# Chunked attention and two dense blocks on one core: the last block's weight residuals on VectorE, and matmuls of zeros at the start

## Chip, core and metric

One core of one Trainium2 chip. The metric is the device time of one execution in microseconds, the median of several; lower is better. TensorE is called PE in the profile, VectorE DVE, ScalarE ACT, GpSimd POOL, and SyncE, which issues all DMA transfers here, SP.

## The reference

Inputs are q, k, v of shape (4, 8, 576, 64), float32. Attention stays inside chunks of 64 positions. Its output, as 2304 tokens of 512 features, goes through two dense blocks with 512 -> 2048 -> 512 weights:

```python
scores = scale * np.matmul(q_c, k_c.transpose(0, 1, 2, 4, 3))   # per chunk of 64
attn = softmax(scores)
x = transpose(attn @ v_c)                       # (2304, 512)
h = x @ w_in;   g = h * np.clip(h + 3.0, 0.0, 6.0) / 6.0;               x = g @ w_out
h = x @ w_in2;  g = np.maximum(h, 0.0) + np.log1p(np.exp(-np.abs(h)));  return g @ w_out2
```

## The kernel before

**Pieces and steps.** The tokens are cut into five pieces: piece 0 of 256 tokens, pieces 1 to 4 of 512. The hidden dimension of 2048 is cut into 16 slices f of 128. A step is one (layer, piece, f): `first_product` (L786) makes 128 hidden rows of h for the piece with 12 matmuls, `activate` (L811) turns them into g, and `second_product` (L896) adds the slice's share of the output with up to 12 more. Products are made of two float32r parts each: every operand is split into a high part and the remainder, and hi·hi, lo·hi and hi·lo are added up. For weights, `split` (L337) makes `wh` by a copy on ACT and `wl` by the subtraction w - wh (`less`, L267). wh0 and wl0 belong to the first product's weights, wh1 and wl1 to the second's. The first product needs wh first (L796) and wl in its last four matmuls (L803). For the second product the output is a PSUM bank per 128 tokens: y for 512-token pieces, z for piece 0 (L922).

**The order of the steps** is written at L743 to L754. The one that matters is the end, layer 2: pieces 1, 2 and 3 one after another, 16 slices each, and then, called the last block here, pieces 4 and 0 alternating over f. One round of the last block is a step of 512 tokens and one of 256. On PE the first product of a step runs two steps ahead of the second one (L1055 to L1068).

**The softplus of layer 2** in the last block (L838 to L882): ACT takes abs of h (L844), exp (L853) and Ln (L856). DVE makes d (L859), l - d (L864), r = min(l, 0) + r (L868). In the 512-token step a separate `top` = max(h, 0) is taken from PSUM (L849) and added (L874); in the 256-token step one instruction does both (L879). Then ACT copies g into gh (L263) and gl = g - gh is made on POOL or DVE (L268).

**Who decides the order on the engines.** The program creates jobs and `Schedule.run` (L58) places them: it simulates engines with estimated costs, picks for each engine the job with the earliest due time among those that are ready, and for a job that can run on several engines (`either`, L257) the first listed engine that meets the due time. The result is one fixed instruction list per engine, which runs in order; the semaphores are added from data and buffer dependences. In this model instructions marked as shared on DVE and POOL exclude each other (`begin`, L101).

**The start.** DMA loads q and k of pieces 0 and 1 (`load_nat`, L985). PE transposes them with an identity matrix, for piece 0 at L423, for piece 1 at L430; ACT copies the result to `qkT`; scores follow at L469; softmax uses DVE and ACT. The weights arrive as raw words, and ACT (L302, L305), DVE (L308 to L319) and POOL (L325) convert them; the first block of them is loaded during the attention.

Of the kernel before, what the change touches and what calls it, by code (L numbers as in the profile page):

```python
# [8 lines left out]
F32 = mybir.dt.float32  # L9
F32R = mybir.dt.float32r  # L10
# [160 lines left out]
def kernel(  # L171
# [18 lines left out]
    nc = tc.nc  # L190
    B, H, S, D = q.shape
    NT, DM = out.shape
    DFF = w_in1.shape[1] // 2
    P = 128
# [12 lines left out]
    NPC = len(pieces)  # L207
# [18 lines left out]
    sch = Schedule(bufs)  # L226
# [12 lines left out]
    def act(n, sbuf=False, wide=False):  # L239
        return {"ACT": ((0.205 if sbuf else 0.170) + 0.000833 * n + (0.03 if wide else 0.0), False)}  # L240

    def dve(n, shared=False):
        return {"DVE": (0.155 + n / 960.0, shared)}
# [4 lines left out]
    def pool(n):  # L248
        return {"POOL": (0.205 + 0.00209 * n, True)}
# [4 lines left out]
    def sp(n_bytes, rate):  # L254
        return {"SP": (n_bytes / rate, "dma")}

    def either(*ons):  # L257
        return {e: c for on in ons for e, c in on.items()}


    def copy(e, out, in_):
        if e == "ACT":
            nc.scalar.activation(out=out, in_=in_, func=AF.Copy)  # L263
        else:
            nc.vector.tensor_copy(out, in_)

    def less(e, out, in0, in1):  # L267
        (nc.vector if e == "DVE" else nc.gpsimd).tensor_tensor(out=out, in0=in0, in1=in1, op=ALU.subtract)  # L268
# [65 lines left out]
        w_done[layer, f, i] = sch.job(total, pool(DM), (c, b), (g, w))  # L334
        return ld

    def split(layer, f, i, before):  # L337

        w = w_buf[layer, f, i]
        hi, lo = (Buf(f"{m}{i}", [P, DM], F32R, f"{m}{i}") for m in ("wh", "wl"))  # L340
        a = sch.job(
            lambda e: copy(e, hi.tile, w.tile.bitcast(F32)),
            act(DM, True), (w_done[layer, f, i], before), (w, hi),
        )
        b = sch.job(
            lambda e: less(e, lo.tile, w.tile.bitcast(F32), hi.tile.bitcast(F32)),
            either(pool(DM), dve(DM, True)), (a,), (w, hi, lo),
        )
        return hi, lo, a, b

# [9 lines left out]
    def load_v(x, c, deps=(), due=1e9):  # L360

        t = Buf("x4_1" if (x, c) == (1, 1) else "v", [P, 2, DM], F32, "v")
        for g in range(2):
            for off, m, b, s in runs(x, (2 * c + g) * P, P):
                def load(e, off=off, m=m, b=b, s=s, g=g):
                    nc.sync.dma_start(  # L366
                        out=t.tile[off:off + m, g, :].rearrange("p (h d) -> p h d", h=H),
                        in_=v[b, :, s:s + m, :].rearrange("h p d -> p h d"),
                    )
                v_load.setdefault((x, 2 * c + g), []).append(sch.job(load, sp(m * DM * 4, 218e3), deps, (t,)))  # L370
            v_buf[x, 2 * c + g] = t
# [3 lines left out]
    class Unit:  # L375
# [34 lines left out]
        def load_nat(self, nat):  # L410

            qkT = Buf(("qkT", "raw"), [P, 2, 512], F32, "qkT")
            self.turned = []
            for y in range(2):
                buf, loads = nat[y]
                t = Buf(self.banks, [P, 512], F32, "pb")

                def turn(e, buf=buf, t=t):
                    if self.x == 0:
                        for u, pr in enumerate(self.prs):  # L420
                            for g in range(2):
                                c = (u * 2 + g) * P
                                nc.tensor.transpose(  # L423
                                    t.tile[:, c:c + P], buf.tile[:, g, pr * P:(pr + 1) * P], ident
                                )
                        return
                    cols = t.tile.rearrange("p (n e) -> p n e", e=4)
                    for g in range(4):
                        for par in range(2):
                            nc.tensor.matmul(  # L430
                                out=cols[par * CH:(par + 1) * CH, :, g],
                                lhsT=buf.tile[:, 2 * self.prs[0] + par, g * D:(g + 1) * D], rhs=ident,
                                start=True, stop=True,
                            )
                a = sch.job(
                    turn, {"PE": (0.53 if self.x == 0 else 1.0, False)}, list(loads) + [made_ident], (buf, t)
                )
                self.turned.append(sch.job(
                    lambda e, t=t, y=y: copy(e, qkT.tile[:, y, :], t.tile),
                    either(act(512), dve(512)), (a,), (t, qkT),  # L440
                ))
            self.qkT = qkT
# [320 lines left out]
    def when(layer, x, nth=0):  # L763
        return [s.at for s in steps if (s.layer, s.x) == (layer, x)][nth]
# [3 lines left out]
    last_split = [None, None]  # L768
# [8 lines left out]
    def weights(s, i):  # L777

        key = s.layer, s.f
        if set_now.get(i, (None,))[0] != key:  # L780
            hi, lo, a, b = split(s.layer, s.f, i, last_split[i])
            last_split[i] = a
            set_now[i] = key, (hi, lo, a, b)
        return set_now[i][1]
# [197 lines left out]
    nat0 = [Buf(t, [P, 2, DM], F32, "nat") for t in ("x2_0", "raw")]  # L982
    nat1 = [Buf(t, [P, H, 4 * D], F32, "nat") for t in ("x2_1", "x3_0")]

    def load_nat(buf, src, x, hs):  # L985

        (b, s, m), = pieces[x]
        nh = hs.stop - hs.start
        if x:
            def load(e):  # L990
                nc.sync.dma_start(
                    out=buf.tile[:, hs], in_=src[b, hs, s:s + m, :].rearrange("h (p e) d -> p h (e d)", p=P)
                )
            return [sch.job(load, sp(m * nh * D * 4, 340e3), (), (buf,))]
        got = []
        for g in range(m // P):
            def load(e, g=g):
                nc.sync.dma_start(
                    out=buf.tile[:, g, hs.start * D:hs.stop * D].rearrange("p (h d) -> p h d", d=D),
                    in_=src[b, hs, s + g * P:s + (g + 1) * P, :].rearrange("h p d -> p h d"),  # L1000
                )
            got.append(sch.job(load, sp(P * nh * D * 4, 218e3), (), (buf,)))
        return got

    first = when(1, 0)
    for u in range(2):
        un = Unit(0, (2 * u, 2 * u + 1), first - 0.3, ("y0", "y1", "y2", "y3", "A0", "H0", "A1", "H1"), True)
        hs = slice(4 * u, 4 * u + 4)
        un.load_nat([
            (nat0[y], load_nat(nat0[y], src, 0, hs))  # L1010
            for y, src in enumerate((q, k))
        ])
    load_v(0, 0)
    for un in units:
        un.attend()
    join = when(1, 1)
    for u in range(NP):
        un = Unit(1, (u,), join - 0.3, ("A0", "y0", "y1", "y2", "y3"), True)
# [17 lines left out]
    before = [j for un in units for j in un.turned]  # L1036
    for x in range(2, NPC):
        a, b = when(1, x - 1), when(1, x)
# [5 lines left out]
        for un in us:  # L1044
            un.load(before)
            before = un.loads
# [8 lines left out]
    for i in range(-2, NS):  # L1055
        if i + 2 < NS:
            s = steps[i + 2]
# [51 lines left out]
```

## Time and profile before

| | |
|---|---|
| time, median of 3 (lowest to highest) | 875.54 us (874.14 to 876.92) |
| profiled execution | 875.73 us |
| its span, first to last instruction | 873.9 us |
| busy: PE, DVE, ACT, POOL | 854.6, 606.5, 539.7, 443.9 us |
| mean granted TensorE clock | 0.994 |

The span is what the trace covers; the time holds 1.8 us more. A busy PE means that matmuls are in flight, not that they follow each other as fast as they can: their ends are modelled. The granted clock is a share of 2.4 GHz. A bracket at the end of a row tells how long the engine stood idle before it and which instruction or transfer ended that.

### The profile page before, as it was taken

To read this page: it belongs to the slowest core of one execution; us is meant where nothing else is said; L and a number is where in the kernel's file an instruction comes from. 1 tells how busy PE (TensorE), PEld (TensorE's weight loads), DVE (VectorE), ACT (ScalarE), POOL (GpSimd) and SP (SyncE) were. 2 spreads that over 40 slices of the span, in tenths; PEclk is the share of its full clock that TensorE was granted. 3 is DMA by queue.
4 is the path that set the end of the run, shared out by engine and by line. 5 is a ranking of instruction groups with operands and counts; after the bars stand their busy time and mean duration, and the time that the engine had idled before them with its cause. 6 is when DMAs were issued, how large, how long until landed. Compare 5 with 4: busy or idle time off the path is not lost.

```text
span 873.9 us, 13785 instructions
## 1 busy us (share of the span) xinstructions
PE 854.6 (98%) x5112; PEld 707.8 (81%) x5112; DVE 606.5 (69%) x951; ACT 539.7 (62%) x993; POOL 443.9 (51%) x349
## 2 busy tenths in 40 slices
PE   7899999999999999999999999999999999999996
PEld 6778788888888888888887888888888888888885
DVE  4898899966554645489788555655565556877775
ACT  4865566455444555488777666666666666565654
POOL 0256454644444444479986444444444444655451
PEclk9899999999999999999999999999999999999999
DMA  9872444142112300046730000100010001000002
GB/s 228 269 203 71 147 123 121 25 74 45 23 23 41 66 25 25 20 154 190 209 128 1 1 1 0 49 1 1 0 49 1 1 0 49 1 1 1 1 0 73
DMA packets 101571, 53.33 MB, mean 61 GB/s; under 512 B 76672, under 2 KB 95104, under 8 KB 101504
## 3 DMA queue, kind: packets, MB, share of 16 engines
q1 hardware_dynamic: 101504, 52.45, 22.0%
q8 instruction: 40, 0.66, 0.3%
q14 instruction: 27, 0.22, 0.1%
HBM read 47.71 MB, written 4.72 MB: 60 GB/s over the span
## 4 chain that ended last, share of the span: by engine, by line
PE 73%; DVE 10%; ACT 5%; SPq 4%; POOL 3%; DMA 2%; issue 2%; DVEq 0%; POOLq 0%; ACTq 0%
PE y L922 33%; PE h L796 24%; PE h L803 12%; DVE r L868 3%; PE z L922 2%; DVE l L864 2%; POOL wl L268 2%; DVE r L874 1%; POOL gl L268 1%; ACT r L853 1%; DMA raww<-in_moe_w_in_dram 1%; SPq L395 1%; ACT l L856 1%; ACT r L844 1%; SPq L366 1%
## 5 line engine op out<-in xcount | busy, mean ns | idle before, releaser
L268 POOL TENSOR_TENSOR wl<-w,wh 128x512 fp32r<-128x512 f32 x249 | 329.4, 1325 | 303.8 <-ACT wh L263 235.3
L796 PE MATMUL h<-x,wh 128*128 128x512 f32 (+1 forms) x1280 | 291.4, 370 | 3.0 <-DVE r L834 2.0
L796 PEld LDWEIGHTS h<-x,wh 128*128 128x128 f32 x1280 | 226.3, 189 | 46.6 <-DVE r L834 3.0
L263 ACT ACTIVATE wh<-w 128x512 fp32r<-128x512 f32 x256 | 160.6, 628 | 109.7 <-PE y L922 61.6
L803 PE MATMUL h<-x,wl 128*128 128x512 f32 (+1 forms) x640 | 159.5, 371 | 0.0
L803 PEld LDWEIGHTS h<-x,wl 128*128 128x128 f32 x640 | 113.3, 189 | 19.9
L325 POOL TENSOR_TENSOR w<-w,cg 128x512 int32<-128x512 int32 x64 | 86.2, 1351 | 77.0 <-DVE cg L319 61.5
L263 ACT ACTIVATE gh<-h 128x512 fp32r<-128x512 f32 x96 | 57.4, 597 | 63.5 <-DVE h L879 34.0
L268 DVE TENSOR_TENSOR gl<-h,gh 128x512 fp32r<-128x512 f32 x96 | 66.1, 688 | 43.5 <-ACT gh L263 42.5
L859 DVE TENSOR_SCALAR d<-r 128x512 f32<-128x512 f32 x80 | 33.2, 415 | 75.9 <-ACT r L853 75.8
L868 DVE SCALAR_TENSOR_TENSOR r<-l,r 128x512 f32<-128x512 f32 x80 | 76.6, 958 | 4.8
L834 DVE SCALAR_TENSOR_TENSOR h<-r,h 128x512 f32<-128x512 f32 x48 | 33.2, 692 | 65.6 <-ACT r L827 65.6
L922 PE MATMUL y<-wh,gh 128*128 128x512 f32 x256 | 72.4, 396 | 1.6 <-ACT gh L263 1.0
L922 PE MATMUL y<-gh,wl 128*128 128x512 f32 x256 | 71.4, 393 | 0.2 <-POOL wl L268 0.2
L922 PE MATMUL y<-gl,wh 128*128 128x512 f32 x256 | 70.8, 391 | 0.0
L922 PE MATMUL y<-gh,wh 128*128 128x512 f32 x256 | 70.8, 391 | 0.0
L922 PE MATMUL y<-wl,gh 128*128 128x512 f32 x256 | 70.5, 390 | 0.0
L922 PE MATMUL y<-wh,gl 128*128 128x512 f32 x256 | 70.5, 390 | 0.0
L827 ACT ACTIVATE r<-h 128x512 f32<-128x512 f32 (+1 forms) x80 | 44.1, 552 | 37.0 <-PE h L803 36.8
L263 ACT ACTIVATE gh<-r 128x512 fp32r<-128x512 f32 (+1 forms) x64 | 33.4, 522 | 53.1 <-DVE r L874 22.9
L864 DVE TENSOR_TENSOR l<-l,d 128x512 f32<-128x512 f32 x80 | 53.6, 670 | 14.7 <-ACT l L856 12.8
L922 PEld LDWEIGHTS y<-wh,gh 128*128 128x128 f32 x256 | 47.4, 188 | 15.8 <-ACT gh L263 5.5
(90 smaller groups left out, 1134.6 us busy)
## 6 DMA issues: line engine op xcount, KB each, us to landing
raww<-in_moe_w_in_dram SPq DMA_DIRECT2D x32, 512.0 KB, 3.9
raww<-in_moe_w_out_dram SPq DMA_DIRECT2D x32, 512.0 KB, 4.6
v<-in_v_dram SPq DMA_DIRECT2D x16, 256.0 KB, 4.5
out_dram<-o SPq DMA_DIRECT2D x16, 256.0 KB, 2.0
raw<-in_q_dram SPq DMA_DIRECT2D x32, 64.0 KB, 3.3
raw<-in_k_dram SPq DMA_DIRECT2D x32, 64.0 KB, 2.5
nat<-in_q_dram SPq DMA_DIRECT2D x4, 256.0 KB, 4.2
nat<-in_k_dram SPq DMA_DIRECT2D x4, 256.0 KB, 4.5
```

Source lines behind the costliest of these rows:

```text
L263: nc.scalar.activation(out=out, in_=in_, func=AF.Copy)
L268: (nc.vector if e == "DVE" else nc.gpsimd).tensor_tensor(out=out, in0=in0, in1=in1, op=ALU.subtract)
L325: nc.gpsimd.tensor_tensor(out=w.tile, in0=w.tile, in1=g.tile.bitcast(I32), op=ALU.add)
L366: nc.sync.dma_start(out=t.tile[off:off + m, g, :].rearrange("p (h d) -> p h d", h=H), in_=v[b, :, s:s + m, :].rearrange("h p d -> p h d"),)
L796: nc.tensor.matmul(out=h.tile[:, :n], lhsT=hi.tile[:, kk * P:(kk + 1) * P], rhs=x.tile[:, kk, :], start=(kk == 0 and m == 0), stop=False,)
L803: nc.tensor.matmul(out=h.tile[:, :n], lhsT=lo.tile[:, kk * P:(kk + 1) * P], rhs=xh.tile[:, kk, :], start=False, stop=(kk == KD - 1),)
L827: nc.scalar.activation(out=of(r), in_=of(h), func=AF.Relu, bias=3.0)
L834: lambda e: nc.vector.scalar_tensor_tensor(out=of(g), in0=of(r), scalar=6.0, in1=of(h), op0=ALU.min, op1=ALU.mult), dve(n), (j,), (h, r), due,
L859: lambda e: nc.vector.tensor_scalar(out=of(d), in0=of(r), scalar1=1.0, scalar2=1.0, op0=ALU.add, op1=ALU.subtract), dve2(n), (u,), (r, d),
L864: lambda e: nc.vector.tensor_tensor(out=of(l), in0=of(l), in1=of(d), op=ALU.subtract),
L868: lambda e: nc.vector.scalar_tensor_tensor(out=of(r), in0=of(l), scalar=0.0, in1=of(r), op0=ALU.min, op1=ALU.add), dve(n, not stays), (j,) ...
L922: nc.tensor.matmul(out=bank.tile[:, col:col + width], lhsT=lhs, rhs=rhs, start=(s.first and m == 0 and opens), stop=(s.last and m == 2 and ...
```

## The change

Two things. In the last block the subtraction that makes wl has to run on DVE; before, POOL came first and DVE second in the list. This holds for every split that a step of piece 0 or 4 in layer 2 asks for: 16 slices of two weights, 32 instructions. And at the start a buffer of zeros is made on DVE, six 128x512 matmuls of it go ahead of everything on PE, and a seventh goes between the transposes of q and of k in the first unit. Their results are not used.

```diff
-    def split(layer, f, i, before):
+    def split(layer, f, i, before, beside):
...
         b = sch.job(
             lambda e: less(e, lo.tile, w.tile.bitcast(F32), hi.tile.bitcast(F32)),
-            either(pool(DM), dve(DM, True)), (a,), (w, hi, lo),
+            dve(DM, True) if beside and layer == 2 else either(pool(DM), dve(DM, True)), (a,), (w, hi, lo),
         )
...
-            hi, lo, a, b = split(s.layer, s.f, i, last_split[i])
+            hi, lo, a, b = split(s.layer, s.f, i, last_split[i], s.x in (0, NPC - 1))
...
+    zero, cold = Buf("gl", [P, 512], F32R, "zero"), Buf("H1", [P, 512], F32, "cold")
+    none = sch.job(lambda e: nc.vector.memset(zero.tile.bitcast(F32), 0.0), {"DVE": (0.485, False)}, (), (zero,), 0.0)
+
+    def warm(n, deps, due):
+        def run(e):
+            for _ in range(n):
+                nc.tensor.matmul(out=cold.tile, lhsT=zero.tile[:, :P], rhs=zero.tile, start=True, stop=True)
+        return sch.job(run, {"PE": (0.44 * n, False)}, deps, (zero, cold), due)
+
+    warm(6, [none], 0.0)
...
+        if u == 0:
+            warm(1, un.turns[:1], 0.0)
```

`un.turns` holds the transposing jobs of a unit, the one of q first. In the changed kernel the lines up to 412 keep their numbers, those of `load_nat` are one higher, those from there to `activate` two higher (L844 becomes L846, L868 becomes L870).

The list of PE before, at its beginning:

```order
L423 MATMUL pb<-ident,nat 128x128 x8
L430 MATMUL pb<-ident,nat 64x128 x8
L469 MATMUL ss<-qkT 64x64 x16
```

And of the change:

```order
L994 MATMUL cold<-zero 128x512 x6
L424 MATMUL pb<-ident,nat 128x128 x4
L994 MATMUL cold<-zero 128x512
L424 MATMUL pb<-ident,nat 128x128 x4
L431 MATMUL pb<-ident,nat 64x128 x8
```

Seven matmuls are added; all the rest of PE's list, and that of SP, is in the same order as before.

The list of DVE before, one round in the middle of the last block, with the engines that each instruction waits for:

```order
L849 TENSOR_SCALAR top<-h 128x512 [waits PE_49]
L859 TENSOR_SCALAR d<-r 128x512 [waits Activation_49]
L864 TENSOR_TENSOR l<-l,d 128x512 [waits DVE_49,Activation_49]
L868 SCALAR_TENSOR_TENSOR r<-l,r 128x512 [waits DVE_49,Pool_49]
L874 TENSOR_TENSOR r<-top,r 128x512 [waits DVE_49]
L859 TENSOR_SCALAR d<-r 128x256 [waits Activation_49]
L864 TENSOR_TENSOR l<-l,d 128x256 [waits DVE_49,Activation_49]
L868 SCALAR_TENSOR_TENSOR r<-l,r 128x256 [waits DVE_49,Pool_49]
L879 SCALAR_TENSOR_TENSOR r<-h,r 128x256 [waits DVE_49]
```

And of the change, the same round from its d on (w_7_0 is slice 7 of the first product's weights, w_6_1 slice 6 of the second's):

```order
L866 TENSOR_TENSOR l<-l,d 128x512 [waits DVE_49,Activation_49]
L870 SCALAR_TENSOR_TENSOR r<-l,r 128x512 [waits DVE_49,Pool_49]
L876 TENSOR_TENSOR r<-top,r 128x512 [waits DVE_49]
L268 TENSOR_TENSOR wl_8102<-w_7_0_4710,wh_8096 128x512 [waits PE_49,Activation_49]
L861 TENSOR_SCALAR d<-r 128x256 [waits Activation_49]
L866 TENSOR_TENSOR l<-l,d 128x256 [waits DVE_49,Activation_49]
L870 SCALAR_TENSOR_TENSOR r<-l,r 128x256 [waits DVE_49,Pool_49]
L881 SCALAR_TENSOR_TENSOR r<-h,r 128x256 [waits DVE_49]
L268 TENSOR_TENSOR wl_8137<-w_6_1_4808,wh_8125 128x512 [waits Activation_49]
L851 TENSOR_SCALAR top<-h 128x512 [waits Activation_49]
```

Two wl stand in each round, and top waits for ACT, whose abs reads the same bank of h, where it waited for PE. POOL's list, which had wl, gl of 512, wl, gl of 256 in a round, keeps the two gl.

The list of ACT before, in the same place:

```order
L263 ACTIVATE gh<-r 128x512 [waits DVE_49]
L263 ACTIVATE wh_8033<-w_5_1_4747 128x512 [waits PE_49]
L263 ACTIVATE gh<-r 128x256 [waits DVE_49]
L844 ACTIVATE r<-h 128x512 [waits DVE_49,Pool_49]
L853 ACTIVATE r<-r 128x512 [waits Activation_49]
```

And of the change:

```order
L263 ACTIVATE gh<-r 128x512 [waits DVE_49]
L263 ACTIVATE wh_8043<-w_5_1_4757 128x512 [waits PE_49]
L263 ACTIVATE gh<-r 128x256 [waits DVE_49]
L846 ACTIVATE r<-h 128x512 [waits PE_49,Pool_49]
L855 ACTIVATE r<-r 128x512 [waits Activation_49]
```

The order is the same; abs of the 512-token step waits for PE and POOL instead of DVE and POOL.

## Rows read from the trace of the kernel before

**Rows 1.** The page, busy us (share of the span) and instructions of each engine.

```profile
PE 854.6 (98%) x5112; PEld 707.8 (81%) x5112; DVE 606.5 (69%) x951; ACT 539.7 (62%) x993; POOL 443.9 (51%) x349
```

**Rows 2.** Timeline of PE, last block: start us, us, engine, line, instruction, count [idle].

```profile
762.51 1.07 PE L922 MATMUL y<-wh,gh 128*128 128x512 f32 x4
...
770.77 1.07 PE L922 MATMUL y<-wh,gh 128*128 128x512 f32 x4
...
779.06 1.19 PE L922 MATMUL y<-wh,gh 128*128 128x512 f32 x4
...
787.68 1.20 PE L922 MATMUL y<-wh,gh 128*128 128x512 f32 x4
...
856.43 1.07 PE L922 MATMUL y<-wh,gh 128*128 128x512 f32 x4
...
863.08 0.50 PE L922 MATMUL y<-wh,gh 128*128 128x512 f32 x1 [0.95 <-ACT gh L263]
```

**Rows 3.** Groups by line and shape, 735 to 862 us: count, busy us, mean ns, idle before.

```profile
L268 POOL TENSOR_TENSOR wl<-w,wh 128x512 fp32r<-128x512 f32 x28 | 39.4, 1407 | 21.7 <-ACT wh L263 21.7
...
L868 DVE SCALAR_TENSOR_TENSOR r<-l,r 128x256 f32<-128x256 f32 x15 | 22.8, 1517 | 1.5
...
L868 DVE SCALAR_TENSOR_TENSOR r<-l,r 128x512 f32<-128x512 f32 x15 | 19.6, 1303 | 1.5
...
L268 POOL TENSOR_TENSOR gl<-r,gh 128x256 fp32r<-128x256 f32 x15 | 11.1, 738 | 1.6 <-ACT gh L263 1.6
```

**Rows 4.** Timeline of all engines, block's start and one round of the last block.

```profile
731.00 0.69 DVE L868 SCALAR_TENSOR_TENSOR r<-l,r 128x512 f32<-128x512 f32 x1
...
796.39 1.30 POOL L268 TENSOR_TENSOR gl<-r,gh 128x512 fp32r<-128x512 f32 x1 [2.08 <-ACT gh L263]
796.42 1.54 DVE L868 SCALAR_TENSOR_TENSOR r<-l,r 128x256 f32<-128x256 f32 x1
...
799.12 0.60 ACT L844 ACTIVATE r<-h 128x512 f32<-128x512 f32 x1 [0.24 <-POOL wl L268]
...
801.64 1.29 POOL L268 TENSOR_TENSOR wl<-w,wh 128x512 fp32r<-128x512 f32 x1 [1.83 <-ACT wh L263]
...
801.88 1.61 DVE L868 SCALAR_TENSOR_TENSOR r<-l,r 128x512 f32<-128x512 f32 x1
```

**Rows 5.** Timeline of ACT, abs of four 512-token steps of the last block.

```profile
737.93 0.60 ACT L844 ACTIVATE r<-h 128x512 f32<-128x512 f32 x1 [0.42 <-PE h L803]
...
773.25 0.60 ACT L844 ACTIVATE r<-h 128x512 f32<-128x512 f32 x1 [0.24 <-POOL wl L268]
...
790.50 0.60 ACT L844 ACTIVATE r<-h 128x512 f32<-128x512 f32 x1 [0.24 <-POOL wl L268]
...
858.21 0.58 ACT L844 ACTIVATE r<-h 128x512 f32<-128x512 f32 x1
```

**Rows 6.** Source view of the subtraction, DVE: count, ns min/median/max, first and last start, forms.

```profile
L268 DVE TENSOR_TENSOR wl<-w,wh x7: 677/679/680, 45.1 to 176.3; 128x512 fp32r<-128x512 f32 x7
```

**Rows 7.** Timeline of PE, transposes of piece 1 and scores at the start.

```profile
6.75 1.98 PE L430 MATMUL pb<-ident,nat 128*64 128x128 f32 x16 [0.38 <-DMA nat<-in_q_dram]
8.66 1.72 PE L469 MATMUL ss<-qkT 64*64 64x64 f32 x32
10.31 1.09 PE L430 MATMUL pb<-ident,nat 128*64 128x128 f32 x16
...
18.17 1.15 PE L469 MATMUL ss<-qkT 64*64 64x64 f32 x32
```

**Rows 8.** Timeline of ACT, the first conversion of weights.

```profile
20.28 0.69 ACT L302 ACTIVATE cg<-raww 128x512 f32<-128x512 f32 x1 [1.31 <-DMA raww<-in_moe_w_in_dram]
```

**Rows 9.** Windows: length, busy us (count) of PE, PEld, DVE, ACT, POOL, granted clock, DMA share, GB/s.

```profile
0.00:10.00 10.00, 5.71 (x50) 4.29 (x52) 0.00 (x0) 3.07 (x4) 0.70 (x6) 1.00 0.82 207
...
30.00:40.00 10.00, 8.92 (x121) 7.59 (x121) 7.18 (x19) 7.06 (x17) 1.30 (x1) 0.66 0.87 270
```

**Rows 10.** Timeline of all engines, output copies at the end.

```profile
865.73 0.69 DVE L265 COPY o<-y 128x512 f32<-128x512 f32 x1
...
869.60 0.60 ACT L263 ACTIVATE o<-y 128x512 f32<-128x512 f32 x1 [0.90 <-DMA out_dram<-o]
```

More of the change, by code (lines that the diff above doesn't have):

```diff
@@ L412, in load_nat @@
             qkT = Buf(("qkT", "raw"), [P, 2, 512], F32, "qkT")
-            self.turned = []
+            self.turned, self.turns = [], []
             for y in range(2):
@@ L437, in load_nat @@
                 )
+                self.turns.append(a)
                 self.turned.append(sch.job(
```

## The prediction

> **What bounds the kernel now.** Start with the page's busy line: TensorE is busy 98% of the span [rows 1]. That is no proof that it runs at its own pace, since the ends of matmuls are modelled. So read next the timeline of TensorE alone in the last block, where it works through 16 rounds, each of a 512-token step, whose second product goes to y, and a 256-token step, whose second product goes to z. The first group of y products starts at 762.51, 770.77, 779.06 and 787.68 us [rows 2]. The rounds are 8.26, 8.29 and 8.62 long, and the work in them is the same. From 770.77 to 856.43 there are ten rounds in 85.66 us; at 8.26 they would take 82.60. **So 3.06 us are lost inside matmuls that count as busy**, and before the last round another 0.95 us as plain idle time, waiting for ACT's gh [rows 2].
>
> Then read who sets the 8.62: all engines in one of those rounds [rows 4]. The abs on ACT of one 512-token step, at 799.12, follows the one at 790.50 by 8.62 us [rows 4, 5], and the way round is ACT abs, exp, Ln, then on VectorE l, r, the sum with top, then d, l, r and the last sum of the 256-token step, then top, then abs again. Two links are too long. The 512-wide r takes 1.61 us, because it overlaps the POOL wl that began 0.24 us earlier; the 256-wide r takes 1.54 us, beside the POOL gl that began 0.03 us earlier [rows 4]. VectorE gets through when POOL's instruction ends. Grouped over the block, the 512-wide r averages 1.303 us and the 256-wide one 1.517 [rows 3]; alone, at the block's start, the 512-wide r takes 0.69 [rows 4]. And abs starts 0.24 us after ACT is free, since it also waits for top: the instruction list has it wait for VectorE, and the wl that the row names ends at about the same moment [rows 4].
>
> Why does TensorE feel this only from 779 us on? The abs of the first round is at 737.93, that of the fifth at 773.25 [rows 5]: 35.32 us for four rounds, against 33.04 of TensorE's work. The loop fell 2.28 us behind before TensorE stalled. That cushion, spent in before, is the figure to keep. It checks: 15 rounds at 0.36 too long is 5.4, less 2.28 is 3.1, the loss found above.
>
> **The low parts on VectorE.** 32 subtractions leave POOL, where they average 1.407 us in this block [rows 3], and go to VectorE, where the same operation, shape and types took 0.677 us in seven cases earlier in this kernel [rows 6]. In the new order one stands behind the 512-wide sum with top, the other behind the last sum of the 256-token step; top now follows abs instead of preceding it. The loop changes at three places:
> - the 512-wide r has no POOL instruction beside it: 1.61 becomes 0.69, so 0.92 less;
> - abs no longer waits for top: 0.24 less;
> - the new wl lies in the loop, 0.68 and a gap of a few hundredths, but the 256-wide part behind it is held by the POOL gl in any case until that ends. If the gl now catches l instead of r, what is added is the step from l to r, about 0.5; if nothing is hidden, 0.70.
>
> The loop becomes 8.62 - 0.92 - 0.24 + 0.5 = about 8.0, at worst 8.2. Both are below 8.26, so TensorE sets the pace, and the cushion of 2.28 stands behind it. The second wl comes after everything the next abs needs; VectorE's own work in a round, some 6.1 us, fits as well. **Term 1: -3.06.** From below it is 0, from above it cannot be more, as the rounds cannot be shorter than 8.26. I take the upper end because the worst loop is still under the pace of TensorE.
>
> **The last round.** The abs of the last step starts at 858.21 [rows 5], 1.78 after the matmuls it reads should be through (856.43, when the y products behind them start), and 863.08 - 858.21 = 4.87 us later TensorE goes on [rows 2]. With the loop on time abs starts about 856.5 and gh is there at 861.4, before TensorE is through with its queue (863.08 - 0.95 = 862.13). **Term 2: -0.95.** Behind it, the output copy of the third y bank on VectorE starts 2.65 us after the first y product [rows 2, 10]; it was slowed by gl, which came as late as gh. With gl there in time, twelve products at the normal pace give the copy about 0.35 sooner, and the last copy on ACT, which waits for an output transfer to free its buffer [rows 10], follows. **Term 3: -0.35**, bounds 0 and -0.4.
>
> **The zeros.** A memset on VectorE, six 128x512 matmuls before the first transposes and one more between those of q and of k. VectorE does nothing in the first 10 us [rows 9], so the memset (at most 0.69) costs nothing there. At TensorE's higher level four such matmuls show 1.07 us [rows 2]; at the lower one at most 0.54 each, so six from about 1.3 us end by 4.5, and the seventh adds 0.54. The transposes may come 0.9 late; 0.38 of that is covered by TensorE's wait for q at 6.75 [rows 7], the rest by the cover of the next paragraph. What they give: the granted-clock column says 1.00 for the first 10 us [rows 9], but the same 16 matmuls take 1.98 us at 6.75 and 1.09 at 10.31, and 32 score matmuls 1.72 at 8.66 and 1.15 at 18.17 [rows 7]. I trust the durations: until shortly before 10 us TensorE runs at 1.2 GHz. At 2.4 it would save 0.89 + 0.57 = 1.46 us. But ACT stands idle 1.31 us until 20.28, waiting for the first block of weights from DMA [rows 8]; what queues behind it there, the copies of turned q and k and an exp, gates VectorE and TensorE. The DMA queue issues without a pause up to there; its list of waits names TensorE only for later blocks of weights, 0.6 us in all. A lead of 1.46 makes ACT wait longer, and if the transposes were 0.5 late ACT would wait less. **Term 4: 0**, bounds -1.46 and +0.1.
>
> Sum: 3.06 + 0.95 + 0.35 = 4.36. The profiled execution took 875.73 (span 873.9 and 1.8 around it); that is 0.2 over the median of 875.54. **875.73 - 4.36 = 871.4 us.**
>
> **Rivals.**
> A. *The lead at the start arrives.* If the weights land earlier, or the idle time on ACT is shorter in other executions, up to 1.46 us come on top: 871.4 - 1.46 = 869.9. For it: VectorE is nearly without gaps behind the first scores, so an earlier start could carry. Against it: the ACT row at 20.28, whose releaser is a transfer. The Trainium skill ("TensorE: Matmul & The Clock Gate", Part 1, "What's actually happening") says that the slow clock is the default and activity releases it, so by that page the zeros do bring the higher level forward and the gain at the head of the kernel would be there to have; the matmul durations agree that the head runs slowly, no row shows that it would reach the end.
>
> B. *No gain in the rounds.* VectorE and POOL hold each other up, and the work is only shifted: the block keeps 8.62 per round. For it: both remaining POOL instructions, 1.30 and 0.74 [rows 3, 4], still stand beside VectorE work, and every low part on VectorE is one more instruction to be held. Time: 875.7, or with the end alone 874.4. The Trainium skill ("Perfetto Trace Analysis", "Optimizing Scalar/DVE Operations") speaks for this rival: moving work between GpSimd and VectorE "might not help", as they share a read port. Against it the rows: the same operation costs 1.407 there and 0.677 here [rows 3, 6], and in the loop a hold of 0.92 goes.
>
> C. *VectorE becomes the bound: slower.* Its queue in a round is 6.1 us of work; eleven gaps of 0.07 make 6.9; if POOL's gl of 512 and of 256 each hold it for their full 1.30 and 0.74, the round is 8.9. Then 15 rounds lose 0.64 each, 9.6 less the cushion of 2.28 is 7.3, against the 3.06 of now: 875.7 + 4.2 = about 880. It decides from a round of 8.8 on: (8.8 - 8.26) x 15 - 2.28 - 3.06 = 2.8. Against it: POOL's 256-wide gl falls where VectorE works on top, which reads PSUM, or waits for ACT.
>
> D. *The clock falls elsewhere.* Between 30 and 40 us the granted clock averages 0.66 [rows 9], after a stretch in which TensorE mostly waited. If the lead turns into more waiting before that, a second such fall could cost about what this one does, 10 x (1 - 0.66) = 3.4 us of TensorE's pace, some 3 of it on the path: 874.4.
>
> **How the numbers follow.** Forecast 0.60, A 0.17, B 0.12, D 0.06, C 0.05. A difference under 0.3%, 2.6 us, cannot be told from none here. Forecast and A are faster by more: 0.77. B and D end within 2.6 us of 875.5: 0.18. C is slower: 0.05. The range reaches from A with a little more, 869.0, to half of term 1 being lost and D, 874.2; it leaves out C, most of B.
>
> **What would show it.** Right: the y groups of the last block start 8.26 us apart to the end; the 512-wide r averages near 0.7 instead of 1.303; no wait for gh before the last round; wl on VectorE near 0.7 to 1.0; the early matmuls at 6.75 and 8.66 take 1.1 us, and ACT's wait at 20.28 has grown by as much. Wrong: rounds above 8.4, the r rows still above 1.2, or ACT's wait at 20.28 gone with the work behind it earlier, which would mean that the lead arrives.

## The result, and the profile after

| | before | after |
|---|---|---|
| time, median (lowest to highest), 4 runs each, side by side | 876.12 us (874.14 to 876.92) | 869.11 us (868.23 to 869.34) |
| ratio, with its 95% interval | | 0.9916 (0.9893 to 0.9938) |
| profiled execution | 875.73 us | 868.23 us |
| its span | 873.9 us | 866.4 us |

The change is faster by 7.0 us. The forecast was 871.4, a gain of some 4.4, in a range from 869.0 to 874.2. At 869.11 the time stands at the fast edge of that range, beside a before of 876.12; on the 875.54 that the forecast started from, the ratio gives 868.2, below the range. So the sign was right, and the gain was forecast about 2.6 us too small. Where does that come from? Cut the span at the first y group of the last block.

The page after, busy time of the engines (answers to [rows 1]):

```profile
PE 850.5 (98%) x5119; PEld 706.8 (82%) x5119; DVE 608.1 (70%) x983; ACT 540.0 (62%) x994; POOL 407.8 (47%) x317
```

POOL has lost 36 us, VectorE gained 1.6, although it took over 32 subtractions: what it no longer loses to being held pays for nearly all of them. One instruction more has changed engine: at the start of the last block an output copy that VectorE made is now on ACT, here and with the low parts alone, but not with the zeros alone. It belongs to the low parts in all that follows; what it is worth by itself was not measured. TensorE is at 98% as before; this line cannot show what was gained.

Timeline of TensorE after, the y groups of the last block (start us, us, engine, line, instruction, count; answers to [rows 2]):

```profile
734.73 1.07 PE L924 MATMUL y<-wh,gh 128*128 128x512 f32 x4
742.99 1.07 PE L924 MATMUL y<-wh,gh 128*128 128x512 f32 x4
...
842.11 1.07 PE L924 MATMUL y<-wh,gh 128*128 128x512 f32 x4
850.37 1.07 PE L924 MATMUL y<-wh,gh 128*128 128x512 f32 x4
855.91 0.39 PE L924 MATMUL y<-wh,gh 128*128 128x512 f32 x1
```

Fourteen rounds of 8.26 to the hundredth, each group 1.07 where it was 1.19, and no bracket before the last one. From the first y group to the last it is 121.18 us; before it was 863.08 - 737.73 = 125.35 (the first y group of before starts at 737.73). From the last group to the end of the span: 866.4 - 855.91 = 10.49, before 873.9 - 863.08 = 10.82. **The tail gave 4.17 + 0.33 = 4.50 us. The head, up to the first y group, gave 737.73 - 734.73 = 3.00 us**, and there the forecast had put nothing.

Groups by line and shape after, 735 to 862 us (answers to [rows 3]):

```profile
L268 DVE TENSOR_TENSOR wl<-w,wh 128x512 fp32r<-128x512 f32 x27 | 26.9, 996 | 1.4 <-ACT wh L263 0.2
L268 POOL TENSOR_TENSOR gl<-r,gh 128x512 fp32r<-128x512 f32 x14 | 20.7, 1475 | 77.9 <-ACT gh L263 77.9
...
L268 POOL TENSOR_TENSOR gl<-r,gh 128x256 fp32r<-128x256 f32 x15 | 17.2, 1149 | 2.2 <-issue 2.2
...
L870 DVE SCALAR_TENSOR_TENSOR r<-l,r 128x512 f32<-128x512 f32 x15 | 10.4, 692 | 1.5
...
L870 DVE SCALAR_TENSOR_TENSOR r<-l,r 128x256 f32<-128x256 f32 x15 | 6.4, 425 | 1.6
```

Both r take what they take alone: 692 ns where it was 1303, 425 where it was 1517. VectorE and POOL still hold each other, but elsewhere. The timeline of all engines in one round shows where (answers to [rows 4, 5]):

```profile
797.09 0.69 DVE L268 TENSOR_TENSOR wl<-w,wh 128x512 fp32r<-128x512 f32 x1
...
798.81 0.42 DVE L870 SCALAR_TENSOR_TENSOR r<-l,r 128x256 f32<-128x256 f32 x1
...
798.90 2.62 POOL L268 TENSOR_TENSOR gl<-r,gh 128x512 fp32r<-128x512 f32 x2 [5.64 <-ACT gh L263]
...
799.61 1.32 DVE L268 TENSOR_TENSOR wl<-w,wh 128x512 fp32r<-128x512 f32 x1
...
801.07 0.60 ACT L846 ACTIVATE r<-h 128x512 f32<-128x512 f32 x1 [0.93 <-PE h L805]
...
801.70 0.69 DVE L851 TENSOR_SCALAR top<-h 128x512 f32<-128x512 f32 x1 [0.77 <-ACT r L846]
```

The two gl run one after the other and catch the round's second wl, which takes 1.32 instead of 0.69. The 256-wide r just escapes them: it starts 0.09 us before the first gl (798.81 and 798.90), where before it started 0.03 behind it [rows 4]. Nothing in the loop waits for the wl: abs now waits 0.93 us for TensorE and top 0.77 for abs. The loop through ACT and VectorE has that much to spare.

Timeline of TensorE at the start after (answers to [rows 7]):

```profile
1.45 2.93 PE L994 MATMUL cold<-zero 128*128 128x512 f32 x6 [1.45 <-DVE zero L989]
4.18 1.05 PE L424 MATMUL pb<-ident,nat 128*128 128x128 f32 x4
4.88 0.78 PE L994 MATMUL cold<-zero 128*128 128x512 f32 x1
5.46 1.15 PE L424 MATMUL pb<-ident,nat 128*128 128x128 f32 x4
6.54 1.09 PE L431 MATMUL pb<-ident,nat 128*64 128x128 f32 x16
7.56 1.15 PE L471 MATMUL ss<-qkT 64*64 64x64 f32 x32
```

The zeros do what they say: the 16 transposing matmuls take 1.09 instead of 1.98 and the first 32 scores 1.15 instead of 1.72, the durations of TensorE's higher level, and the first scores start at 7.56 instead of 8.66. Timeline of ACT, its first conversion of weights (answers to [rows 8]), and the window from 30 to 40 us (length, busy us of PE, PEld, DVE, ACT, POOL, granted clock, DMA share, GB/s; answers to [rows 9]):

```profile
18.95 0.68 ACT L302 ACTIVATE cg<-raww 128x512 f32<-128x512 f32 x1 [1.65 <-DMA raww<-in_moe_w_in_dram]
```

```profile
30.00:40.00 10.00, 9.24 (x105) 6.91 (x103) 9.90 (x21) 8.84 (x20) 3.99 (x3) 1.00 0.89 245
```

ACT waits longer, 1.65 instead of 1.31, yet the transfer it waits for landed 1.33 earlier; and the granted clock stays at 1.00 where it averaged 0.66. Neither need come from the zeros. So the first question was which half of the change gives what, and how far two executions of one kernel differ in the head.

### The profile page after: what moved, and what is told of

Same layout as the page of the kernel before. It is cut to its first block, busy times and chain, and to the rows that moved or that the text cites. A ratio compares the mean times of both kernels' runs of the same rounds, so it can differ in the third digit from the quotient of the medians.

```text
span 866.4 us, 13798 instructions
## 1 busy us (share of the span) xinstructions
PE 850.5 (98%) x5119; PEld 706.8 (82%) x5119; DVE 608.1 (70%) x983; ACT 540.0 (62%) x994; POOL 407.8 (47%) x317
## 4 chain that ended last, share of the span: by engine, by line
PE 89%; DVE 5%; ACT 2%; DMA 2%; issue 1%; POOL 1%; DVEq 0%; SPq 0%; ACTq 0%; POOLq 0%
PE y L924 38%; PE h L798 29%; PE h L805 15%; PE z L924 4%; DMA raww<-in_moe_w_in_dram 1%; DVE p L483 1%; PE ss L471 1%; PE oo L648 1%; PE st L608 1%; PE oo L522 1%; PE st L615 1%; DVE cg L319 1%; DVE x L268 0%; PE cold L994 0%; DVE p L492 0%
## 5 line engine op out<-in xcount | busy, mean ns | idle before, releaser
L268 POOL TENSOR_TENSOR wl<-w,wh 128x512 fp32r<-128x512 f32 x217 | 284.0, 1311 | 283.0 <-ACT wh L263 216.2
L268 POOL TENSOR_TENSOR gl<-r,gh 128x512 fp32r<-128x512 f32 (+1 forms) x30 | 38.7, 1306 | 88.3 <-ACT gh L263 86.1
L866 DVE TENSOR_TENSOR l<-l,d 128x512 f32<-128x512 f32 x80 | 51.4, 643 | 15.3 <-ACT l L858 14.8
L846 ACT ACTIVATE r<-h 128x512 f32<-128x512 f32 x80 | 44.4, 554 | 21.9 <-PE h L805 21.9
```

The costliest lines, as they stand in the source:

```text
L846: j = sch.job(lambda e: nc.scalar.activation(out=of(r), in_=of(h), func=AF.Abs), act(n), (s.h_done,), (h, r))
L866: lambda e: nc.vector.tensor_tensor(out=of(l), in0=of(l), in1=of(d), op=ALU.subtract),
```

## The experiments

Every kernel of this section computes the whole reference.

**The two halves, and both kernels again (one chip).** The zeros alone; the low parts alone; and one more execution of each kernel of the pair, with no edit.

```diff
 e1_zeros_only: the change, with
-            dve(DM, True) if beside and layer == 2 else either(pool(DM), dve(DM, True)), (a,), (w, hi, lo),
+            either(pool(DM), dve(DM, True)), (a,), (w, hi, lo),
 e2_wl_only: the change, without
-    warm(6, [none], 0.0)
-        if u == 0:
-            warm(1, un.turns[:1], 0.0)
```

> Only the zeros; the low parts stay where they were. Theory 1 (both parts pay, and add): the head is 3.0 us shorter, as the first y group of the last block shows (734.73 against 737.73 us in the two profiles), the last block keeps rounds of 8.62 us; time 3.0 us under before, 872.5 to 873.3. Theory 2 (the head of the changed kernel was only lucky in its profiled execution, and ACT's wait for weights absorbs the lead as predicted): 0 to 0.5 us under before. Theory 3 (lead of 1.5 us arrives, the absence of the second clock fall is chance): 1.3 to 1.7 us under before. In the profile theory 1 wants no stretch at 1.2 GHz near 30 us and the first matmul of the first dense block near 29.3 us.

> Only the low parts on VectorE, no zeros. Theory 1: the last block runs at 8.26 us per round to its end, no wait for gh before the last round: 4.4 to 4.5 us under before, 871.0 to 872.0. Theory 2 and 3 say the same of this part and want the rest of the 7 us from elsewhere: if this kernel alone is 6 us or more under before, the zeros do nothing.

> The kernel before, once more, for its trace. Theory 1: ACT's first conversion of weights starts near 20.3 us and the clock falls to 1.2 GHz near 30 us again. Theory 2: one or both of them differ by a microsecond or more from the first profile, as they vary by chance.

> The changed kernel, once more, for its trace. Theory 1: the clock rises near 6.5 us and does not fall until the end; ACT's first conversion starts near 19 us. Theory 2: the clock falls in this execution in the waiting stretch between 24 and 29 us, or the conversion starts near 20.3 us, and the time is about the same all the same.

Measured: zeros alone 873.21 us, ratio to before 0.9966 (0.9953 to 0.9978); low parts alone 870.37, 0.9946 (0.9927 to 0.9965); one execution of before 875.06, of the change 870.5. Theory 1 has the time of the zeros alone, but not its signs: there the first product of the dense block starts at 30.66 us, and the granted clock from 30 to 40 us is 0.83.

The tail belongs to the low parts alone. Timeline of TensorE with the low parts alone, y groups:

```profile
734.33 1.07 PE L922 MATMUL y<-wh,gh 128*128 128x512 f32 x4
...
849.97 1.07 PE L922 MATMUL y<-wh,gh 128*128 128x512 f32 x4
855.51 0.39 PE L922 MATMUL y<-wh,gh 128*128 128x512 f32 x1
```

855.51 - 734.33 = 121.18, the change's value to the hundredth. With the zeros alone, y groups of TensorE and groups by line:

```profile
776.72 1.20 PE L924 MATMUL y<-wh,gh 128*128 128x512 f32 x4
785.36 1.19 PE L924 MATMUL y<-wh,gh 128*128 128x512 f32 x4
...
860.83 0.50 PE L924 MATMUL y<-wh,gh 128*128 128x512 f32 x1 [0.94 <-ACT gh L263]
```

```profile
L268 POOL TENSOR_TENSOR wl<-w,wh 128x512 fp32r<-128x512 f32 x27 | 38.0, 1410 | 20.9 <-ACT wh L263 20.9
L870 DVE SCALAR_TENSOR_TENSOR r<-l,r 128x256 f32<-128x256 f32 x14 | 21.2, 1515 | 1.5
L870 DVE SCALAR_TENSOR_TENSOR r<-l,r 128x512 f32<-128x512 f32 x15 | 20.9, 1392 | 1.5
```

Rounds of 8.64, both r held, and the wait for gh, as in [rows 2 to 4]. **So the zeros touch only the head, and there they are worth something: 0.34% of the time, where the forecast had 0.**

How much of the 3.00 us of the profiled pair is that? The first y group starts at 737.73 in the first execution of before and at 736.98 in the second; at 734.73 and 737.04 in the two of the change; at 734.33 with the low parts alone. The head differs by 2 us and more between executions of one kernel. One place shows it well, the first products of the dense block on TensorE. In the change's first execution and in its second:

```profile
29.27 1.22 PE L798 MATMUL h<-x,wh 128*128 128x256 f32 x8
```

```profile
31.30 2.07 PE L798 MATMUL h<-x,wh 128*128 128x256 f32 x8
```

The second one runs them at the lower level, as the first execution of before did (2.07, window 0.66). The second execution of before has no fall (1.22, window 1.00). That the clock stayed up in the change's first execution was chance.

**The clock near 30 us.** Is it the fall there that costs, and do the zeros prevent it? In these kernels 18 matmuls of zeros, 128x256, fill TensorE's waits between 26 and 32 us; once on before, without zeros at the start, once on the change.

```diff
+        n_pe, last_oo, FILL = 0, None, {24: 10, 25: 4, 26: 4}
...
+                for _ in range(FILL.get(n_pe, 0)):
+                    nc.tensor.matmul(
+                        out=last_oo.tile[:, HALF:], lhsT=zero.tile[:, :P], rhs=zero.tile[:, :HALF], start=True, stop=True
+                    )
```

> Before, with zeros only in the stretch near 27 to 31 us where TensorE waits (10, 4 and 4 matmuls of 128x256 around the last products of the attention), none at the start. Theory F (the zeros of the change pay by keeping the clock from falling near 30 us, which cost 2.1 us between two matmuls 20 apart in the first trace): no stretch at 1.2 GHz near 30 us in the trace, time 1.0 to 2.5 us under before. Theory L (they pay by the early rise, the lead at the start arrives): at most 0.7 us under before, as only some executions of before have the fall. If the added matmuls get in the way of the last products: above before.

> The change with the same zeros in the waiting stretch on top. Theory F: as the changed kernel without a fall, 868 to 869 in all executions, no better than its best. Theory L: 0 to 0.7 us under the change (869.1 to 868.4), for those executions that still have the fall (one of the two traces of the change has it).

Measured: on before 874.3 us, ratio 0.9989 (0.9975 to 1.0003), beside 875.21; on the change 869.33, 0.9928 (0.9911 to 0.9944). The clock does stay up; window 30 to 40 us of the first one:

```profile
30.00:40.00 10.00, 8.91 (x134) 7.22 (x131) 9.02 (x22) 9.11 (x20) 2.56 (x2) 1.00 0.95 258
```

On before it is worth 0.9 us, with an interval from -0.3 to 2.2, so theory F, which wanted 1.0 to 2.5, is not excluded by this run alone. On the change it is worth nothing: 869.33, with executions from 868.01 to 871.30, where F wanted 868 to 869 in all. So the fall near 30 us alone does not explain the gain.

**ACT's wait for the first weights.** Term 4 rests on it. Here the first two conversions of weights move back in the lists of ACT, VectorE and POOL, so that ACT has other work until the transfer is there; once with the zeros, once without.

```diff
+        for group, on, start, behind in (
+            (split0, "ACT", made[1, 1, 0][0], 3), (made[1, 0, 0][2:], "DVE", made[1, 0, 0][4], 4),
+            (made[1, 0, 0][:2], "ACT", made[1, 0, 0][0], 4), (made[1, 1, 0], "ACT", made[1, 1, 0][0], 8),
+        ):
...
+            order = head + moved + order[order.index(later) + 1:]
```

> The change, with the conversions of the first two blocks of weights moved back in the lists of ACT, VectorE and POOL, behind the work of the attention that now stands behind them, so that ACT does not wait for the transfers near 20 and 26 us. Theory G (these waits take back part of the lead that the zeros give): ACT's waits of 1.6 to 2.6 and 0.5 to 1.3 us go, the first matmul of the first dense block starts 0.5 to 1.5 us earlier than the 29.3 to 31.3 of the traces with zeros, time 0.3 to 1.5 us under the change. Rival W (what counts in the head is when the weights of the first slices are converted, or their transfers further on): no gain or up to 1 us above the change, although the matmul at 29 us is earlier.

> The same move without the zeros, beside the kernel with the low parts alone (870.4). Theory G: the waits it removes are small without the lead (0 to 1.3 and 0 to 0.6 us in three traces without zeros), so 0 to 0.5 us, less than in the kernel with zeros; the difference between this and the one with zeros is then the full lead, 2 us or more. Rival W: the same difference between the two as before the move, 1.3 us.

Measured: with the zeros 870.16 us, ratio 0.9934 (0.9919 to 0.9949), without 872.04, 0.9955 (0.9938 to 0.9972). The wait is gone; timeline of ACT with the zeros:

```profile
21.39 0.70 ACT L302 ACTIVATE cg<-raww 128x512 f32<-128x512 f32 x1
```

Theory G fails: both kernels came out slower than without the move (869.11 and 870.37, on other chips). With zeros it is still 1.9 us faster, with an interval of about 1.1 to either side, which holds both the 2 of theory G and the 1.3 of rival W. That the lead brings more without that wait is not shown.

**The lead put back.** If the lead of the first scores is what pays, a delay of the same size must cost the same. Six or twelve more matmuls of zeros go ahead of the first scores, where the clock is already up; beside them on one chip the change and the low parts alone, without edits.

```diff
             def scores(e):
+                if x == 0 and self.prs[0] == 0:
+                    for _ in range(6):
+                        nc.tensor.matmul(out=s.tile, lhsT=zero.tile[:, :P], rhs=zero.tile, start=True, stop=True)
                 for c in range(nch):
```

> The low parts on VectorE and no zeros, once more, on one chip with the change. Theory L (the lead of the zeros arrives): 2.0 to 2.5 us slower than the change. Theory S (ACT's wait for the weights absorbs the lead, and the earlier difference was scatter): no slower than the change by more than 0.5 us. Its tail has rounds of 8.26 under both.

> The change once more, the reference of the three others of this set: about 869 us.

> The change with six more 128x512 matmuls of zeros ahead of the first scores, at the higher clock: some 1.6 us of delay, as much as the zeros bring forward. Theory L: the delay arrives, time 1.3 to 1.7 us above the change, near the kernel without zeros. Theory S: ACT waits less for its first weights and the time stays within 0.4 us of the change.

> The same with twelve matmuls, some 3.2 us of delay. Theory L: 2.6 to 3.3 us above the change. Theory S: 1.5 to 2 us above the change, since only what goes beyond ACT's wait of 1.3 to 1.8 us arrives.

Measured: low parts alone 870.24 us, ratio to before 0.9932 (0.9916 to 0.9947); the change 868.45, 0.9918 (0.9901 to 0.9934); with six 868.77, 0.9923 (0.9908 to 0.9937); with twelve 869.28, 0.9926 (0.9912 to 0.9941). The delay is there; with six, timeline of TensorE and of ACT:

```profile
6.69 1.09 PE L431 MATMUL pb<-ident,nat 128*64 128x128 f32 x16 [0.54 <-DMA nat<-in_q_dram]
7.71 1.65 PE L468 MATMUL ss<-zero 128*128 128x512 f32 x6
9.29 1.15 PE L473 MATMUL ss<-qkT 64*64 64x64 f32 x32
```

```profile
19.39 0.68 ACT L302 ACTIVATE cg<-raww 128x512 f32<-128x512 f32 x1 [0.35 <-DMA raww<-in_moe_w_in_dram]
```

The first scores start at 9.29, later than in before (8.66), ACT's wait shrinks to 0.35, and the end moves by 0.3 us. With twelve, a delay of over 3 us costs 0.8, with an interval of about 0.9 to either side. **Theory L falls for these delays: the head has slack for most of such a shift.** Theory S fits with six; with twelve it wanted 1.5 to 2 us, more than was measured; and the low parts alone are 1.8 us slower, between the 0.5 of S and the 2.0 of L. The chain of waits that ended last, asked for the head alone, is in line with slack. In before (start us, us, what), and with the six matmuls:

```profile
17.65 2.27 SPq L366
19.97 1.40 SPq L366
21.41 4.83 DMA raww<-in_moe_w_in_dram
...
32.97 2.37 SPq L395
35.38 1.62 SPq L395
37.05 2.30 SPq L395
```

```profile
27.50 0.69 DVE p L494
28.19 0.59 DVE sm L501
...
31.22 2.00 PE h L800 x8
```

In before the chain up to 41 us is made mostly of DMA transfers and of their issues on SP; in the other of VectorE and TensorE. Two chains of nearly the same length run beside each other, so a shift of one can be hidden by the other. Which of them ends last is not a matter of the kernel: the second run of the zeros alone has the transfers' chain, and the second of the low parts alone, without zeros, has mostly that of the engines up to 28 us.

How a lead is lost can be followed, since TensorE's list is the same in all these kernels but for the zeros. The change's first product of the dense block starts at 29.27, as shown above. The same product with the low parts alone (timeline of TensorE), and from the chains the group of y products some 33 us later, of the change and of the low parts alone:

```profile
31.61 1.22 PE L796 MATMUL h<-x,wh 128*128 128x256 f32 x8
```

```profile
62.25 2.11 PE y L924 x8
```

```profile
62.03 2.11 PE y L922 x8
```

A lead of 2.34 us has become a lag of 0.22. TensorE's waits between 38 and 110 us, of the change and of the low parts alone (us in total, times, longest), name most of what it met there:

```profile
PE h L798 <- DVE r L836: 2.4, 4, 0.8
PE y L924 <- ACT wh L263: 0.6, 1, 0.6
```

```profile
PE h L796 <- DVE r L834: 1.0, 2, 0.6
```

From that y group to the end of the span it is 804.2 us in the change and 804.0 in the other. **So in this pair the lead of the first 30 us is lost at waits for VectorE and ACT before 62 us.** The fall of the clock goes the same way: in the two executions of before, the first with it and the second without, this group starts at 64.11 and 64.31. And the scatter of the end is mostly made ahead of it: in the fourteen traces with the low parts on VectorE it starts between 62.0 and 65.1, and what follows takes 803.9 to 805.6.

**Zeros without a lead.** The zeros alone again, with and without the six matmuls of delay (low parts on POOL); and, with the low parts on VectorE, seven matmuls of zeros ahead of the first scores and none before, beside the low parts alone. The edits are those above.

> The zeros with the low parts on POOL as before. If the zeros are worth 2 to 2.7 us there: 872.5 to 873.5, beside a kernel before of about 875.5. If they are worth 1.2 as on the last chip: about 874.3.

> The same with six more matmuls of zeros ahead of the first scores, 1.6 us at the higher clock. Theory L (the lead arrives): 1.3 to 1.7 us above the kernel without this delay, near the kernel before. Theory N (the gain does not come through the lead, the head has slack for it): within 0.6 us of the kernel without the delay.

> The low parts on VectorE and seven matmuls of zeros ahead of the first scores alone, none before the transposes: no lead, a delay of 1.9 us at the higher clock to 3.4 at the lower. Theory L: 1.5 to 3.5 us slower than the kernel without zeros. Theory N: within 0.6 us of the change, 0.7 to 1.5 us faster than the kernel without zeros. If it equals the kernel without zeros, the head has slack for a delay and zeros help only where they bring the clock forward.

> The low parts on VectorE and no zeros, the reference of the last one: 870.2, with executions between 867.8 and 873.8.

Measured: zeros alone 873.78 us, ratio to before 0.9982 (0.9968 to 0.9995); with the delay 873.23, 0.9978 (0.9967 to 0.9989); zeros at the scores alone 870.12, 0.9942 (0.9925 to 0.9958); low parts alone 870.08, 0.9948 (0.9928 to 0.9968). The zeros alone are worth less here (0.18%) than on the first chip (0.34%). With the low parts on POOL too the delay takes nothing of the gain away. Zeros that come only at the scores bring nothing that can be seen, and their delay costs nothing; at 8.34 us they still find TensorE at the lower level:

```profile
8.34 3.16 PE L468 MATMUL ss<-zero 128*128 128x512 f32 x7
11.43 1.15 PE L473 MATMUL ss<-qkT 64*64 64x64 f32 x32
```

**The same place, reached in two ways.** Zeros at the start with twelve more at the scores, and seven at the scores alone, have the second scores at 14.49 and 14.55 us in the runs above, and differ only ahead of that. Once more, side by side:

> The change with twelve matmuls of zeros ahead of the first scores, once more, on one chip with the next kernel. If what the zeros do ahead of the scores carries the gain: 0.8 to 1.5 us faster than the next one, about 869.2. If the position of the work carries it: equal to the next one within 0.4 us.

> The low parts on VectorE and seven matmuls of zeros ahead of the first scores alone, once more; its work from 14.5 us on stands where that of the kernel before stands. 870.1 as before if the gain comes from ahead of the scores, about 869.3 like the other if it comes from the position.

Measured: 869.79 us, ratio 0.993 (0.9914 to 0.9946), and 870.35, 0.9936 (0.9921 to 0.9952). A difference of 0.6 us in the same direction as the first time (869.28 and 870.12). But in this pair the second scores start at 14.31 and 14.98, 0.67 apart, so the place was not the same. In the first pair the first dense products still stand level, at 33.23 and 33.29, and the granted clock then averages 0.83 and 0.66 from 30 to 40 us. All executions of the two together, 12 each, differ by 0.7 us in the mean, with an interval of 0.8 to either side: not decided. No kernel here is shown to beat the change.

All runs of the four kernels, over all chips:

| kernel | runs | median | lowest to highest | mean |
|---|---|---|---|---|
| before | 81 | 875.54 | 872.66 to 878.87 | 875.65 |
| zeros alone | 20 | 873.41 | 871.80 to 876.75 | 873.55 |
| low parts alone | 18 | 870.15 | 867.76 to 874.24 | 870.37 |
| the change | 11 | 868.98 | 867.24 to 870.50 | 868.85 |

By the means the low parts give 5.3 us without and 4.7 with zeros (intervals of 0.9 and 0.8 to either side); the zeros 2.1 with the low parts on POOL and 1.5 with them on VectorE (0.6 and 1.0). The profiled executions alone would not show the zeros: the change 868.23, 870.50 and 868.43, the low parts alone 867.76, 868.59 and 871.27.

## Where the prediction was right, and where it failed

**Terms 1 to 3** (3.06 + 0.95 + 0.35 = 4.36) came as forecast: the tail gave 4.50 in the profiled pair, and the low parts 4.7 to 5.3 by the means of the runs. The fourteen rounds of 8.26 take 850.37 - 734.73 = 115.64 us, before 856.43 - 737.73 = 118.70: term 1, 3.06 as forecast. No wait for gh, and the last y group follows the one before by 5.54 us where it was 6.65: term 2, 1.11 where 0.95 was forecast. Last group to end 0.33 shorter: term 3. The runs of the halves show that all of it hangs on the low parts.

Inside term 1 one step was wrong without harm. The loop was sized at 8.0 to 8.2, with the 256-wide r still held by POOL's gl. It is shorter, an estimated 8.26 - 0.77 = 7.5 from top's wait: r of 256 takes 425 ns, since it now starts 0.09 us ahead of the gl, and the second wl is held in its place. That is a small margin, which the forecast did not foresee; had it gone the other way, the loop would by the forecast's own estimate of 8.0 to 8.2 still have been under 8.26. Two more readings were loose. The check of the loss, 15 rounds of 0.36 less 2.28, counts one round too many: between the first y group and the one at 856.43 there are 14, which gives 2.8. And VectorE does not get through when POOL's instruction ends: the 512-wide r of [rows 4] ends at 803.49, 0.56 after POOL's wl, and the 256-wide one at 797.96, 0.27 after POOL's gl. Neither changes a term.

**Rivals B and C** fall: no round is above 8.26, and VectorE's busy time rose by 1.6 us. The Trainium skill ("Perfetto Trace Analysis", "Optimizing Scalar/DVE Operations") says that moving work between GpSimd and VectorE "might not help", since they share a read port. The sharing shows: wl takes 996 ns on average, 1.32 us where it meets gl, and POOL's gl of 256 rose from 738 to 1149 ns. But what counts is which instruction is held. Before it was r, in the loop that sets the round; now it is one that nothing in the loop waits for, and that is worth the 4.5 us.

**Term 4 is the step that failed: "0, bounds -1.46 and +0.1".** The zeros measure -1.5 to -2.1. Its mechanism, that ACT's wait for weights absorbs the lead, was half right: a delay of the first scores by 1.6 us does change little at the end (873.23 beside 873.78, 868.77 beside 868.45). ACT's wait before its first conversion did grow: with zeros it was 1.65, 1.80, 1.40, 2.59 and 2.38 us, without them 1.31, 0.17 and three times none. And in the pair of executions that was followed above, the lead that was left at 29 us was lost before 62 us. But from "the lead is absorbed" the forecast went on to "the zeros give nothing", and it took both from a single execution, whose wait of 1.31 was the longest of those without zeros. The granted clock's fall, too, was a matter of the execution.

**Rival A** gave 869.9, near the result, but by the wrong way: it needs the lead to arrive at the end, and the delays show that it does not have to. **Rival D**, a fall of the clock near 30 us, happens in some executions with and without zeros; keeping it away by filling gave 0.9 on before, with an interval that includes 0, and nothing on the change.

What carries the zeros' 1.5 to 2.1 us stays open. The runs speak against the simple answers: the lead of the first scores (put back, it costs little), ACT's first wait (with it gone, the zeros are worth about as much), the clock near 30 us alone, and TensorE's activity at the scores. A mixture of them, each below what these runs resolve, is not excluded. What the runs suggest, no more: without zeros some executions end late (up to 874.24 with the low parts on VectorE, where the change has none above 870.50), so the zeros may take away the late ones rather than speed up each. With the low parts on POOL this is less clear: there the zeros have an execution of 876.75 too.

## What to carry to other kernels

When two engines hold each other up, look at which instruction is held and who waits for it. Moving the other partner's work so that the loop that sets the pace is no longer held can pay even though the sharing goes on and one engine has more to do: here VectorE took over 32 instructions, and 4.5 us were gained.

A term that rests on one wait in one profiled execution needs that wait's scatter. In a stretch where a transfer chain and a compute chain are nearly level, neither the full lead nor zero is a safe value; widen the range to both. And follow the same instruction through two traces: where their distance changes, the lead is lost or won.

## What had not been expected of the hardware

The moment at which TensorE's clock rises at the start differs between executions of one program. The 16 matmuls behind the first scores took 1.09 us in the first execution of before [rows 7], and in its second:

```profile
10.49 1.90 PE L430 MATMUL pb<-ident,nat 128*64 128x128 f32 x16
```

The Trainium skill ("TensorE: Matmul & The Clock Gate", "What's actually happening") says that the number of slow matmuls at a kernel's start varies from run to run; these two rows agree. That a delay of over 3 us on TensorE, 8 us into the program, costs about 0.8 us at the end was not expected either.
